# A fused attention and maxout kernel whose late output stores are cut differently

## The chip, the cores and the metric

The kernel runs on one core of one Trainium2 chip. The metric is the device time of that core in microseconds; the time before is 161.82 us, the median of three runs that lie between 161.29 and 162.05 us. The execution that was profiled took 162.39 us, and its trace spans 160.6 us of that.

## The reference

Eight batches of an attention with 32 memory slots per head (8 heads, 576 positions, head size 64), and behind it a feed-forward layer with a maximum over three products:

```python
a   = softmax(phi)                            # over the 32 slots
k_m = einsum('bhsm,bhsd->bhmd', a, k)         # 32 keys and 32 values per head
v_m = einsum('bhsm,bhsd->bhmd', a, v)
x   = softmax(q @ k_m.T / sqrt(64)) @ v_m     # [8, 8, 576, 64] -> x [4608, 512]
h   = max(max(x @ w1, x @ w2), x @ w3)        # [4608, 768]
out = h @ w_out                               # [4608, 512], float32
```

## The kernel before, in words

The weights are rewritten once. `max(x w1, x w2, x w3)` is `max(x (w1-w3), x (w2-w3), 0) + x w3`, so `w_diff` (lines 213 to 224, step `V`) subtracts `w3` from `w1` and `w2` in place in `w12`, a view of 4 x 1536 columns, in ranges of 512 columns (`BANK`). `w1` ends at column 768 (`DF`), so the range 512 to 1024 crosses the border between the two weights and is cut into two instructions there by the loop's `e`. `V0` runs on GpSimd, `V1` and `V2` on VectorE.

For each batch the attention is reduced to 32 keys and values per head, the values are folded into the weights (step `D`), and the feed-forward layer is run straight on the attention's probabilities: step `F` (`ffn1`) makes one 128-row slice of `h` transposed, step `T` (`ffn2`, lines 658 to 700) makes 128 rows of the output: six matmuls of `h` with `w_out` and two of the probabilities with the folded `w3 w_out`, summed in one PSUM bank, copied to an SBUF tile `ot` and stored to HBM. Batches 0 and 1 do four such row tiles each, and `T4` of each odd batch does 128 rows that straddle the border of the pair: the last 64 of the even batch and the first 64 of the odd one. Batch 7's `T4` is `ffn2_last` (lines 706 to 741), the last work of the kernel: its 128 rows are made in two halves of 256 columns, each copied and stored by itself, the first through VectorE and SyncE's queue (L737, L738), the second through ScalarE and its own queue (L740, L741).

Batches 2 to 7 make their other 512 rows in another way: a 2 x 2 block product with seven multiplications instead of eight. Steps `U` and `A` form sums of weight and activation blocks, and `products` (step `P`, L615) runs multiplication `i` of seven. The output has two row blocks (`r` = 0, 1; 256 rows each) and two column halves (256 columns each); multiplications 2, 4, 6 and 5 finish the four quarters (4 only when multiplication 3 is there too). Each finished quarter is written to a tile `ot` of its row block by L642 or L647. For batches 2 to 6 one store of 512 KB per row block follows once its second half is there (after 4 and after 6); for batch 7 each quarter is stored at once, 256 KB each:

```python
if n in (4, 6) or b == B - 1:        # line 648
```

The order of the work is written out by hand: the string at lines 782 to 808 is a list of steps, `name@batch`, and every engine executes its own instructions in that order. Near the end the steps that matter here are `P1@6 ... P2@6 ... P1@7 ... P2@7 P5@6 P3@6 ... P4@7 P6@6 P0@7 P5@7 P3@7 P6@7 T4@7`. The `ot` tiles come from a pool of four buffers (`opool`), so a tile's first writers wait until the stores from the tile that had this buffer before have landed. The framework puts in all semaphores. Stores and loads that are issued by SyncE or ScalarE take one of eight completion semaphores in turn; an issue first waits until the transfer that used its semaphore eight issues earlier has landed. In the built program there are 29 such issues: the two loads of `phi` at line 91, four stores of batch 0 on ScalarE's queue (`send`, line 704), 21 stores of line 700 and line 652 on SyncE's queue, and the last two, L738 and L741. At the end of the program SyncE runs nine wait instructions (line 837, the launch line, stands for them), each for two semaphores, in a fixed order; the second to the ninth hold the eight DMA semaphores in their order. A drain and a barrier over all engines follow.

Of the kernel before, what the change touches and what calls it, by code (L numbers as in the profile page):

```python
# [15 lines left out]
def kernel(  # L16
# [12 lines left out]
    nc = tc.nc  # L29

    B, H, S, D = q.shape
# [121 lines left out]
    def one_bank():  # L153
        return psum[:, int(next(banks))]
# [57 lines left out]

    def w_diff(n, swap):

        c, end = n * BANK, (n + 1) * BANK
        while c < end:
            e = min(end, (c // DF + 1) * DF)
            (nc.gpsimd if swap else nc.vector).tensor_tensor(  # L218
                out=w12[:, :, c:e],
                in0=w12[:, :, c:e],  # L220
                in1=w_sb[:, :, 2, c % DF : c % DF + e - c],
                op=ALU.subtract,
            )
            c = e
# [356 lines left out]
    def products(b, i, swap):  # L581

        s, a = sums(b), blocks(b)
        wp3 = wp3s[b]

        def plain(r, c):
            return lambda k, q: a[r][c][:, k, q]

        def summed(n):
            src = a[1][0] if n == 2 else s[min(n, 2)]  # L590
            return lambda k, q: src[:, k, q]

        def w_plain(i, j):
            c = slice(CH * j, CH * (j + 1))
            return lambda k: wo_sb[:, KT * i + k, c] if k < KT else wp3[:, i, c]

        def w_summed(n):
            return lambda k: tw[:, n, k] if k < KT else twb[b % 2][:, n]

        lhs, rhs, name = [  # L600
            (summed(0), w_summed(0), "y"),
            (plain(0, 0), w_plain(0, 0), "x"),
            (plain(0, 1), w_plain(1, 0), "z"),
            (summed(3), w_plain(1, 1), "y"),
            (summed(1), w_summed(1), "x"),
            (summed(2), w_summed(2), "x"),
            (plain(1, 1), w_summed(3), "x"),
        ][i]
        acc = quads.setdefault(b, {})
        if i < 3:  # L610
            acc[name] = one_bank()
        po = acc[name]
        for k in range(KT + 1):
            for q in range(2):
                nc.tensor.matmul(  # L615
                    po[:, q * CH : (q + 1) * CH],
                    lhsT=lhs(k, q),
                    rhs=rhs(k),
                    start=(i < 3 and k == 0 and q == 0),
                    stop=(k == KT and q == 1),  # L620
                    skip_group_check=True,
                )
        x = po.rearrange("p (q n) -> p q n", q=2)

        def copy(out_, in_):
            if swap:
                nc.vector.tensor_copy(out=out_, in_=in_)
            else:
                nc.scalar.copy(out=out_, in_=in_)  # L629

        if i in SNAP:
            t = ln if i == 0 else work.tile([P, S], FP32, name="snap", tag="r")
            t = acc[SNAP[i]] = t[:, 0:DM].rearrange("p (q n) -> p q n", q=2)
            copy(t, x)
        acc[i] = True
        done = [2] if i == 2 else [i] if i > 4 else [4] if 3 in acc and 4 in acc else []
        for n in done:
            if ("ot", n // 5) not in acc:
                acc["ot", n // 5] = opool.tile([P, 2, DM], FP32, name="ot")
            ot = acc["ot", n // 5][:, :, slice(0, CH) if n in (2, 6) else slice(CH, DM)]  # L640
            if n == 6:
                copy(ot, x)  # L642
            else:
                if n == 4:
                    x = acc["y"].rearrange("p (q n) -> p q n", q=2)
                y = acc[{2: "m1", 4: "u2", 5: "m5"}[n]]
                nc.vector.tensor_tensor(out=ot, in0=x, in1=y, op=ADD)  # L647
            if n in (4, 6) or b == B - 1:
                r0 = b * S + (b % 2) * HP
                rows = out[r0 : r0 + 2 * TW].rearrange("(q r p) c -> p q r c", q=2, r=2)  # L650
                c = slice(0, DM) if b < B - 1 else slice(0, CH) if n in (2, 6) else slice(CH, DM)
                nc.sync.dma_start(
                    out=rows[:, :, n // 5, c], in_=acc["ot", n // 5][:, :, c]
                )

    osts = {}

    def ffn2(b, t, swap):


        hT, attn = hts[b // 2], attns[b // 2]
        c0 = S - HP if t == 4 else (b % 2) * (S + HP) + t * P
        if b == B - 1:
            return ffn2_last(b, c0)
        po = one_bank()
        for n, fc in enumerate(fts[b]):
            nc.tensor.matmul(  # L667
                po,
                lhsT=hT[:, row(fc), c0 : c0 + P],
                rhs=wo_sb[:, fc, :],  # L670
                start=(n == 0),
                stop=False,
            )
        for g in range(NG):
            if t < 4:
                nc.tensor.matmul(  # L676
                    po,
                    lhsT=attn[:, g, c0 : c0 + P],
                    rhs=wp3s[b][:, g, :],
                    start=False,  # L680
                    stop=(g == NG - 1),
                )
            else:
                for u in range(2):
                    nc.tensor.matmul(  # L685
                        po[HP * u : HP * (u + 1)],
                        lhsT=attn[:, g, c0 + HP * u : c0 + HP * (u + 1)],
                        rhs=wp3s[b - 1 + u][:, g, :],
                        start=False,
                        stop=(g == NG - 1),  # L690
                        tile_position=(0, HP * u),
                    )
        ot = opool.tile([P, 2, DM], FP32, name="ot")[:, 0]
        r0 = (b // 2) * 2 * S + c0
        rows = out[r0 : r0 + P, :]
        evacuate("T", t, swap, ot, po)
        if b == 0:
            osts[t] = (rows, ot)
        else:
            nc.sync.dma_start(out=rows, in_=ot)  # L700

# [41 lines left out]
    def issue(b, n, swap):  # L743
# [29 lines left out]
            "W": lambda: w3_t(i, swap),  # L773
            "g": lambda: send(i),
            "d": lambda: fold_begin(i),
            "O": lambda: w3_o(i, swap),
            "V": lambda: w_diff(i, swap),
            "Z": lambda: warm_up(i),
# [3 lines left out]
    for w in """  # L782
# [1 line left out]
        M0@0 M1@0 R0@0 R1@0 W0@0 Y3@0 W1@0 W2@0 Z6@0 O1@0 H3@0 O3@0 O2@0 H1@0 X1@0 B1@0  # L784
        X0@0 N1@0 K1@0 O0@0 Y0@0 D1@0! D0@0! D3@0 F8@0 Y1@0 F10@0! L0@1 L1@1 F6@0 J0@1
        F0@0! F2@0! D2@0 D4@0 F4@0 F1@0 F3@0 F5@0 F11@0 F7@0 V0@0! E@1 F9@0 B0@1 N0@1
        T2@0! J1@1 Q0@1 L2@1 Q1@1 V2@0 K0@1! T1@0 S@1 B1@1 V1@0 L3@2 N1@1 M1@1 a0@1 s0@1
        R1@1 c0@1 K1@1 T3@0 D2@1 m0@1! D0@1 X1@1 L1@2 X0@1 D1@1 Q0@2 L0@2 T0@0! L2@2
        L1@3 Q1@2 L0@3 r0@2 F8@1! F4@1 F6@1! F7@1 E@2 F10@1! F2@1 F5@1 F0@1 g2@0 B@2
        D3@1 L2@3 L3@3 N@2 F9@1 F3@1 K@2! F11@1 g1@0 S@2 F1@1 D1@2! E@3 L1@4 U2@9 D0@2  # L790
        D3@2 T3@1 U0@9 T4@1! L0@4 r0@3 a@2 s@2 c@2 D2@2 B@3 L2@4 m@2! U2@2 X@2 F10@2 N@3
        F2@2 F11@2 F4@2 F0@2 K@3! L3@4 Q0@3 Q1@3 F6@2 F1@2 F8@2 g0@0 F3@2 S@3 F7@2 a@3
        F5@2 g3@0 s@3 F9@2 r0@4! E@4 U0@2 c@3 L0@5 U1@9 m@3! T2@1 X@3 U3@9 D0@3 D3@3
        T0@1! T1@1 L1@5 D2@3 B@4 D1@3! N@4 P1@2! L2@5 Q1@4 U1@2 F2@3 F6@3 F3@3 F8@3 L3@5
        U3@2 L1@6 U0@3 A0@2! Q0@4 K@4! F4@3! F0@3 F9@3 P2@2! A1@2! S@4 A2@2! A3@2! F5@3
        E@5 a@4 P4@2 F1@3 r0@5 P0@2 L2@6 F10@3 L0@6 s@4 F7@3 c@4 P5@2 m@4 D1@4! D3@4
        U1@3 F11@3 P3@2 A0@3! D2@4 B@5 A2@3! N@5 D0@4 X@4 T4@3! L1@7 A1@3! F10@4 Q0@5
        K@5 F0@4 L3@6 Q1@5 P6@2! S@5 r0@6! F11@4 F2@4! F1@4 L0@7 F6@4 F4@4! P1@3 F8@4
        a@5 s@5 U2@3 D2@5 D3@5 c@5 P2@3! E@6 m@5 A3@3! F5@4 P4@3 F3@4 F9@4 P0@3 D1@5!
        X@5 B@6 N@6 L2@7 D0@5 P5@3 U3@3 F8@5! F7@4 P3@3! r0@7! L3@7 U0@4 F2@5! F10@5 E@7  # L800
        U0@5 F3@5 Q0@6 A0@4! U1@4 P6@3 F11@5 F4@5 Q1@6 F6@5 F9@5 K@6! F0@5 A2@4! U2@4
        F5@5 S@6 F7@5 A1@4! a@6 A3@4! B@7 N@7 s@6 D3@6 D1@6! P0@4 P1@4 U3@4 K@7! P2@4!
        F1@5 Q1@7 P4@4 c@6 D0@7 D1@7 D0@6 P3@4 P5@4 U0@6 Q0@7 m@6 X@6 D2@6 D3@7 D2@7!
        A0@5! T4@5 S@7 A1@5! P6@4 F0@6 a@7 s@7 F4@6 F10@6 F1@6 c@7 F2@6 U2@5 F6@6 P1@5
        F3@6 F7@6 U1@5 P2@5 F8@6 A3@5! F9@6 F11@6 P4@5 m@7 X@7 F5@6 P0@5! F6@7 F10@7!
        A2@5! F2@7 P3@5! F4@7! F0@7 P5@5 F8@7! F1@7 F11@7 A0@6! U3@5 P6@5 F5@7 F9@7 U0@7
        A1@6 U1@7 A2@6 F3@7 U1@6 P1@6 F7@7 P0@6 P2@6! P4@6 U2@6 P1@7 A0@7 A3@6 U3@6 A1@7
        U3@7! P2@7! P5@6! P3@6 U2@7! A2@7 A3@7 P4@7 P6@6 P0@7! P5@7 P3@7! P6@7 T4@7!
    """.split():
        n, b = w.rstrip("!").split("@")  # L810
        issue(int(b), n, w.endswith("!"))
# [30 lines left out]
```

## Time and profile before

| | |
|---|---|
| median of three runs | 161.82 us (161.29 to 162.05) |
| profiled execution | 162.39 us |
| its span, first to last instruction | 160.6 us |
| TensorE matmul busy | 149.8 us, 93% |
| VectorE, ScalarE, GpSimd busy | 74%, 61%, 65% |
| granted TensorE clock | full in all 40 slices |
| DMA moved | 31.78 MB |

The span leaves out what lies before the first and after the last instruction, 1.8 us in this execution. Busy shares are averages over the whole span; what sets the end is read in the timeline and the waits of the last microseconds.

### The profile page before, as it was taken

Reading aid. Unit: us, or ns where it says so; the run is one execution under the profiler, and the core shown is the slowest. Engines: PE = TensorE matmul, PEld = TensorE weight load, DVE = VectorE, ACT = ScalarE, POOL = GpSimd, SP = SyncE. Lnnn points to the kernel's source line nnn. Section 1 sums busy time; section 2 is a strip of 40 time slices with the busy share of each in tenths; the row PEclk is TensorE's granted clock in tenths of the full one; section 3 lists DMA queues with packets and bytes.
Section 4 is the critical chain, followed back from the end, with each engine's and each line's share of the span. In section 5 each row is a group of like instructions: output and inputs, shape, how many; then the busy total and the mean of one; then the engine's idle time right before and its main releaser. Section 6 shows DMA issues by size and latency. Waiting matters only on the chain.

```text
span 160.6 us, 5165 instructions
## 1 busy us (share of the span) xinstructions
PE 149.8 (93%) x2219; PEld 100.4 (62%) x2228; DVE 118.5 (74%) x205; ACT 98.2 (61%) x140; POOL 104.3 (65%) x98
## 2 busy tenths in 40 slices
PE   7978698979897999999999999999999999999991
PEld 2433444654455537636877577787774888888871
DVE  2023803699897897897998789898989869799851
ACT  3205435742786699997777789888876944224210
POOL 7932101993039949968999996999969996910000
PEclk9999999999999999999999999999999999999999
DMA  5999999999999999999999999999803500330374
GB/s 150 164 201 203 201 209 214 279 207 212 209 276 245 276 233 261 285 262 282 268 231 209 259 260 254 261 173 170 271 0 134 196 6 0 131 131 4 150 279 159
DMA packets 22342, 31.78 MB, mean 198 GB/s; under 512 B 1072, under 2 KB 17456, under 8 KB 22320
## 3 DMA queue, kind: packets, MB, share of 16 engines
q0 software_dynamic: 16096, 21.43, 70.9%
q1 hardware_dynamic: 5504, 8.85, 15.3%
q10 hardware_dynamic: 720, 1.18, 2.2%
q8 instruction: 17, 0.28, 0.7%
q14 instruction: 5, 0.04, 0.1%
HBM read 39.32 MB, written 9.44 MB: 304 GB/s over the span
## 4 chain that ended last, share of the span: by engine, by line
PE 63%; DMA 25%; POOL 6%; issue 2%; ACT 1%; DVE 1%; POOLq 0%
PE psum L504 23%; PE psum L615 23%; DMA w_sb<-in_moe_w_dram 14%; DMA kvr<-in_v_dram 10%; PE psum L667 6%; PE psum L453 4%; PE psum L256 3%; PE psum L342 2%; POOL qq L112 1%; DMA out_dram<-ot 1%; POOL kvr L97 1%; POOL ko L97 1%; PE psum L676 1%; PE psum L685 1%; POOL w_sb L119 1%
## 5 line engine op out<-in xcount | busy, mean ns | idle before, releaser
L504 PE MATMUL psum<-hx,wp 128*128 128x288 bf16 x384 | 53.2, 286 | 0.1
L504 PEld LDWEIGHTS <-wp 128*128 128x128 bf16 x384 | 36.3, 98 | 11.6 <-issue 2.1
L517 DVE TENSOR_TENSOR hx<-psum,h 128x576 bf16<-128x576 f32 x48 | 34.8, 749 | 6.3 <-PE psum L504 4.5
L177 ACT CAST wp<-psum 128x1024 bf16<-128x1024 f32 (+1 forms) x29 | 27.5, 993 | 4.6 <-PE psum L453 4.4
L175 ACT ACTIVATE h<-psum 128x576 bf16<-128x576 f32 x34 | 21.5, 655 | 7.2 <-PE psum L504 6.6
L615 PEld LDWEIGHTS <-hx 128*128 128x128 bf16 x192 | 18.4, 98 | 3.5 <-issue 1.1
L667 PE MATMUL psum<-wo_sb,hx 128*128 128x512 bf16 x60 | 15.6, 380 | 0.3
L351 ACT ACTIVATE e<-psum 128x576 bf16<-128x576 f32 x16 | 9.5, 649 | 6.2 <-PE psum L342 6.2
L164 PE MATMUL psum<-warm 128*128 128x512 bf16 x42 | 12.0, 440 | 1.4 <-DVE warm L131 1.2
L615 PEld LDWEIGHTS <-w_sb 128*128 128x128 bf16 x120 | 11.6, 98 | 2.4 <-issue 0.8
L321 DVE STREAM_TRANSPOSE qT<-qq 128x576 f32<-128x576 f32 x16 | 11.9, 760 | 1.1 <-DMA qq<-in_q_dram 1.0
L107 POOL COPY kvr<-ko 128x2304 bf16<-128x2304 bf16 x3 | 6.3, 2111 | 8.8 <-DMA ko<-in_k_dram 8.8
L629 ACT COPY snap<-psum 128x512 f32<-128x512 f32 x11 | 6.5, 594 | 8.7 <-PE psum L615 8.7
L540 POOL TENSOR_TENSOR w_sb<-hx 128x1024 bf16<-128x1024 bf16 x5 | 10.6, 2121 | 1.6 <-DVE hx L517 1.6
L234 ACT ACTIVATE e<-ph 128x1152 bf16<-128x1152 f32 (+1 forms) x9 | 9.6, 1067 | 2.4 <-DMA ph<-in_phi_dram 2.4
L218 POOL TENSOR_TENSOR w_sb<-w_sb 128x2048 bf16<-128x2048 bf16 x1 | 4.1, 4052 | 10.6 <-PE psum L453 10.6
L179 DVE TENSOR_SCALAR h<-psum 128x576 bf16<-128x576 f32 x14 | 10.3, 746 | 0.7 <-PE psum L504 0.6
L667 PEld LDWEIGHTS <-hx 128*128 128x128 bf16 x66 | 5.9, 98 | 7.5 <-issue 1.7
L256 PEld LDWEIGHTS <-e 64*32 64x32 bf16 x720 | 7.3, 89 | 5.1 <-issue 3.6
L427 POOL TENSOR_TENSOR t<-t,sm 128x1152 bf16<-128x1152 bf16 x4 | 8.5, 2124 | 3.0 <-DVE sm L420 1.7
L540 POOL TENSOR_TENSOR twb<-wp 128x256 bf16<-128x256 bf16 x11 | 7.4, 675 | 4.2 <-ACT wp L177 4.2
L177 ACT COPY ot<-psum 128x512 f32<-128x512 f32 x9 | 5.3, 595 | 7.7 <-PE psum L676 6.8
(102 smaller groups left out, 280.6 us busy)
## 6 DMA issues: line engine op xcount, KB each, us to landing
out_dram<-ot SPq DMA_DIRECT2D x10, 512.0 KB, 3.3
qq<-in_q_dram POOLq DMA_DIRECT2D x7, 576.0 KB, 11.0
ph<-in_phi_dram POOLq DMA_DIRECT2D x7, 576.0 KB, 14.6
ko<-in_k_dram POOLq DMA_DIRECT2D x7, 576.0 KB, 16.6
kvr<-in_v_dram POOLq DMA_DIRECT2D x7, 576.0 KB, 11.1
out_dram<-ot SPq DMA_DIRECT2D x11, 256.0 KB, 6.1
w_sb<-in_moe_w_dram POOLq DMA_DIRECT2D x3, 768.0 KB, 19.0
out_dram<-ot ACTq DMA_DIRECT2D x4, 256.0 KB, 6.8
```

The lines of the kernel that those rows point to most:

```text
L164: nc.tensor.matmul(po[:, 0:BANK], lhsT=warm[:, 0:P], rhs=warm, start=True, stop=True)
L175: nc.scalar.activation(out=out_, in_=in_, func=AF.Relu)
L177: nc.scalar.copy(out=out_, in_=in_)
L179: nc.vector.tensor_scalar_max(out=out_, in0=in_, scalar1=0.0)
L234: nc.scalar.activation(out=s["e"][:, js], in_=loaded[b]["ph"][:, js], func=AF.Exp)
L256: nc.tensor.matmul(kvp[M * j : M * (j + 1), a, 0:nd], lhsT=s["e"][r, j, c, :], rhs={None: lambda: k_and_v(b, r, j, c), 0: lambda: ones_and ...
L321: nc.vector.transpose(out=s["qT"][:, j].rearrange("p j c r e -> p (j c r e)").bitcast(FP32), in_=loaded[b]["q"][:, j].rearrange("p j c d - ...
L504: nc.tensor.matmul(acc[:, h, 0:SH], lhsT=wps[b][:, g, w * DF + ft * P : w * DF + (ft + 1) * P], rhs=attn[:, g, c0 : c0 + SH], start=(g == ...
L517: nc.vector.tensor_tensor(out=hT[:, row(ft), (b % 2) * S : (b % 2 + 1) * S].rearrange("p (h n) -> p h n", h=2), in0=a, in1=s["h1", ft], op ...
L540: eng.tensor_tensor(out=out_, in0=in0, in1=in1, op=op)
L615: nc.tensor.matmul(po[:, q * CH : (q + 1) * CH], lhsT=lhs(k, q), rhs=rhs(k), start=(i < 3 and k == 0 and q == 0), stop=(k == KT and q == 1 ...
L667: nc.tensor.matmul(po, lhsT=hT[:, row(fc), c0 : c0 + P], rhs=wo_sb[:, fc, :], start=(n == 0), stop=False,)
```

## The change

Four edits. The stores of batch 6 are cut like those of batch 7: each finished quarter leaves by itself, so there are four stores of 256 KB instead of two of 512 KB. Row tile 3 of batch 1 is stored in two halves of 64 rows instead of one of 128 rows. A new step `t` (`ffn2_begin`) opens the PSUM bank of a row tile and runs the first four of its matmuls with `w_out`; `ffn2` then goes on with the rest. In the written order every `t` stands directly ahead of its own `T`. The weight difference is written as four ranges that end at the border between the weights, and `V3@0` stands directly behind `V1@0`.

```diff
     def w_diff(n, swap):
-        c, end = n * BANK, (n + 1) * BANK
+        c, end = [(0, BANK), (BANK, DF), (2 * BANK, 2 * DF), (DF, 2 * BANK)][n]
...
-            if n in (4, 6) or b == B - 1:
+            if n in (4, 6) or b >= B - 2:
                 r0 = b * S + (b % 2) * HP
                 rows = out[r0 : r0 + 2 * TW].rearrange("(q r p) c -> p q r c", q=2, r=2)
-                c = slice(0, DM) if b < B - 1 else slice(0, CH) if n in (2, 6) else slice(CH, DM)
+                c = slice(0, DM) if b < B - 2 else slice(0, CH) if n in (2, 6) else slice(CH, DM)
...
+    def ffn2_begin(b, t):
+        po = opened[b, t] = one_bank()
+        hT, c0 = hts[b // 2], (b % 2) * (S + HP) + t * P
+        for n, fc in enumerate(fts[b][0:4]):
+            nc.tensor.matmul(
+                po,
+                lhsT=hT[:, row(fc), c0 : c0 + P],
+                rhs=wo_sb[:, fc, :],
+                start=(n == 0),
+                stop=False,
+            )
...
-        po = one_bank()
-        for n, fc in enumerate(fts[b]):
+        early = (b, t) in opened
+        po = opened[b, t] if early else one_bank()
+        for n, fc in enumerate(fts[b][4 if early else 0 :]):
...
-                start=(n == 0),
+                start=(n == 0 and not early),
...
+        elif (b, t) == (1, 3):
+            for r in (slice(0, HP), slice(HP, P)):
+                nc.sync.dma_start(out=rows[r], in_=ot[r])
         else:
             nc.sync.dma_start(out=rows, in_=ot)
...
-        T2@0! J1@1 Q0@1 L2@1 Q1@1 V2@0 K0@1! T1@0 S@1 B1@1 V1@0 L3@2 N1@1 M1@1 a0@1 s0@1
+        t2@0 T2@0! J1@1 Q0@1 L2@1 Q1@1 V2@0 K0@1! t1@0 T1@0 S@1 B1@1 V1@0 V3@0 L3@2 N1@1
...
-        R1@1 c0@1 K1@1 T3@0 D2@1 m0@1! D0@1 X1@1 L1@2 X0@1 D1@1 Q0@2 L0@2 T0@0! L2@2
+        M1@1 a0@1 s0@1 R1@1 c0@1 K1@1 t3@0 T3@0 D2@1 m0@1! D0@1 X1@1 L1@2 X0@1 D1@1 Q0@2
+        L0@2 t0@0 T0@0! L2@2 L1@3 Q1@2 L0@3 r0@2 F8@1! F4@1 F6@1! F7@1 E@2 F10@1! F2@1
...
+        E@3 L1@4 U2@9 D0@2 D3@2 t3@1 T3@1 U0@9 T4@1! L0@4 r0@3 a@2 s@2 c@2 D2@2 B@3 L2@4
...
+        T2@1 X@3 U3@9 D0@3 D3@3 t0@1 T0@1! t1@1 T1@1 L1@5 D2@3 B@4 D1@3! N@4 P1@2! L2@5
```

(`t2@1` closes the line ahead of the last one shown; the rest of the string is the same list with other line breaks.)

More of the change, by code (lines that the diff above doesn't have):

```diff
@@ L654, in products @@
                 )
-    osts = {}
+    osts, opened = {}, {}
+    def ffn2_begin(b, t):
[9 more added lines that the diff above has]
+            )
     def ffn2(b, t, swap):
@@ L775, in issue @@
             "d": lambda: fold_begin(i),
+            "t": lambda: ffn2_begin(b, i),
             "O": lambda: w3_o(i, swap),
@@ L786 @@
         F0@0! F2@0! D2@0 D4@0 F4@0 F1@0 F3@0 F5@0 F11@0 F7@0 V0@0! E@1 F9@0 B0@1 N0@1
-        T2@0! J1@1 Q0@1 L2@1 Q1@1 V2@0 K0@1! T1@0 S@1 B1@1 V1@0 L3@2 N1@1 M1@1 a0@1 s0@1
-        R1@1 c0@1 K1@1 T3@0 D2@1 m0@1! D0@1 X1@1 L1@2 X0@1 D1@1 Q0@2 L0@2 T0@0! L2@2
-        L1@3 Q1@2 L0@3 r0@2 F8@1! F4@1 F6@1! F7@1 E@2 F10@1! F2@1 F5@1 F0@1 g2@0 B@2
-        D3@1 L2@3 L3@3 N@2 F9@1 F3@1 K@2! F11@1 g1@0 S@2 F1@1 D1@2! E@3 L1@4 U2@9 D0@2
-        D3@2 T3@1 U0@9 T4@1! L0@4 r0@3 a@2 s@2 c@2 D2@2 B@3 L2@4 m@2! U2@2 X@2 F10@2 N@3
@@ L792 @@
[L792 to L808, printed above, removed]
+        t2@0 T2@0! J1@1 Q0@1 L2@1 Q1@1 V2@0 K0@1! t1@0 T1@0 S@1 B1@1 V1@0 V3@0 L3@2 N1@1
@@ new lines @@
+        M1@1 a0@1 s0@1 R1@1 c0@1 K1@1 t3@0 T3@0 D2@1 m0@1! D0@1 X1@1 L1@2 X0@1 D1@1 Q0@2
+        L0@2 t0@0 T0@0! L2@2 L1@3 Q1@2 L0@3 r0@2 F8@1! F4@1 F6@1! F7@1 E@2 F10@1! F2@1
+        F5@1 F0@1 g2@0 B@2 D3@1 L2@3 L3@3 N@2 F9@1 F3@1 K@2! F11@1 g1@0 S@2 F1@1 D1@2!
+        E@3 L1@4 U2@9 D0@2 D3@2 t3@1 T3@1 U0@9 T4@1! L0@4 r0@3 a@2 s@2 c@2 D2@2 B@3 L2@4
+        m@2! U2@2 X@2 F10@2 N@3 F2@2 F11@2 F4@2 F0@2 K@3! L3@4 Q0@3 Q1@3 F6@2 F1@2 F8@2
+        g0@0 F3@2 S@3 F7@2 a@3 F5@2 g3@0 s@3 F9@2 r0@4! E@4 U0@2 c@3 L0@5 U1@9 m@3! t2@1
@@ new lines @@
+        T2@1 X@3 U3@9 D0@3 D3@3 t0@1 T0@1! t1@1 T1@1 L1@5 D2@3 B@4 D1@3! N@4 P1@2! L2@5
+        Q1@4 U1@2 F2@3 F6@3 F3@3 F8@3 L3@5 U3@2 L1@6 U0@3 A0@2! Q0@4 K@4! F4@3! F0@3
+        F9@3 P2@2! A1@2! S@4 A2@2! A3@2! F5@3 E@5 a@4 P4@2 F1@3 r0@5 P0@2 L2@6 F10@3
+        L0@6 s@4 F7@3 c@4 P5@2 m@4 D1@4! D3@4 U1@3 F11@3 P3@2 A0@3! D2@4 B@5 A2@3! N@5
+        D0@4 X@4 T4@3! L1@7 A1@3! F10@4 Q0@5 K@5 F0@4 L3@6 Q1@5 P6@2! S@5 r0@6! F11@4
+        F2@4! F1@4 L0@7 F6@4 F4@4! P1@3 F8@4 a@5 s@5 U2@3 D2@5 D3@5 c@5 P2@3! E@6 m@5
@@ new lines @@
+        A3@3! F5@4 P4@3 F3@4 F9@4 P0@3 D1@5! X@5 B@6 N@6 L2@7 D0@5 P5@3 U3@3 F8@5! F7@4
+        P3@3! r0@7! L3@7 U0@4 F2@5! F10@5 E@7 U0@5 F3@5 Q0@6 A0@4! U1@4 P6@3 F11@5 F4@5
+        Q1@6 F6@5 F9@5 K@6! F0@5 A2@4! U2@4 F5@5 S@6 F7@5 A1@4! a@6 A3@4! B@7 N@7 s@6
+        D3@6 D1@6! P0@4 P1@4 U3@4 K@7! P2@4! F1@5 Q1@7 P4@4 c@6 D0@7 D1@7 D0@6 P3@4 P5@4
+        U0@6 Q0@7 m@6 X@6 D2@6 D3@7 D2@7! A0@5! T4@5 S@7 A1@5! P6@4 F0@6 a@7 s@7 F4@6
+        F10@6 F1@6 c@7 F2@6 U2@5 F6@6 P1@5 F3@6 F7@6 U1@5 P2@5 F8@6 A3@5! F9@6 F11@6
@@ L809 @@
+        P4@5 m@7 X@7 F5@6 P0@5! F6@7 F10@7! A2@5! F2@7 P3@5! F4@7! F0@7 P5@5 F8@7! F1@7
+        F11@7 A0@6! U3@5 P6@5 F5@7 F9@7 U0@7 A1@6 U1@7 A2@6 F3@7 U1@6 P1@6 F7@7 P0@6
+        P2@6! P4@6 U2@6 P1@7 A0@7 A3@6 U3@6 A1@7 U3@7! P2@7! P5@6! P3@6 U2@7! A2@7 A3@7
+        P4@7 P6@6 P0@7! P5@7 P3@7! P6@7 T4@7!
     """.split():
```

## The prediction

> **What bounds the kernel now.** I read the page first: shares of engines, then the chain that ended last.
>
> ```profile
> span 160.6 us, 5165 instructions
> PE 149.8 (93%) x2219; PEld 100.4 (62%) x2228; DVE 118.5 (74%) x205; ACT 98.2 (61%) x140; POOL 104.3 (65%) x98
> PE 63%; DMA 25%; POOL 6%; issue 2%; ACT 1%; DVE 1%; POOLq 0%
> ```
>
> TensorE works through most of the span, so a change pays only if it shortens TensorE's stream, its stalls, or the tail behind its last matmul. The tail is in the timeline from 155 us on.
>
> ```profile
> 155.91 1.48 PE L727 MATMUL psum<-wo_sb,hx 128*128 128x256 bf16 x12
> 156.77 0.42 DVE L737 COPY ot<-psum 128x256 f32<-128x256 f32 x1 [1.56 <-PE psum L727]
> 157.22 0.34 SPq L738 DMA_DIRECT2D out_dram<-ot  x1
> 157.43 0.37 ACT L740 COPY ot<-psum 128x256 f32<-128x256 f32 x1 [1.39 <-DMA out_dram<-ot]
> 157.83 0.34 ACTq L741 DMA_DIRECT2D out_dram<-ot  x1
> ```
>
> The last matmul ends at 157.39, the last copy starts at 157.43, and the last store is issued at 157.83. (The copy's releaser is given as a store. Its two semaphore waits ran at 155.5, long before, so I read the matmul of 157.39 as the releaser.) The page's list of DMA issues gives the landing.
>
> ```profile
> out_dram<-ot SPq DMA_DIRECT2D x10, 512.0 KB, 3.3
> out_dram<-ot SPq DMA_DIRECT2D x11, 256.0 KB, 6.1
> out_dram<-ot ACTq DMA_DIRECT2D x4, 256.0 KB, 6.8
> ph<-in_phi_dram SPq DMA_DIRECT2D x2, 288.0 KB, 3.2
> out_dram<-ot SPq DMA_DIRECT2D x1, 128.0 KB, 1.7
> out_dram<-ot ACTq DMA_DIRECT2D x1, 128.0 KB, 1.7
> ```
>
> 157.83 + 1.7 is 159.53, yet the span ends at 160.6. What fills the last 1.07 us stands in the rows of the launch line: first SyncE from 157.5 to 159.0, then from 159.0 to 159.58, from 159.58 to 159.79, and from 159.79 to 159.9; then the other engines' queues after 158.
>
> ```profile
> L837 SPq EVENT_SEMAPHORE  x5: 28/28/28, 157.6 to 159.0; - x5
> ...
> L837 SPq EVENT_SEMAPHORE  x1: 28/28/28, 159.5 to 159.5; - x1
> ...
> L837 SPq EVENT_SEMAPHORE  x3: 28/28/28, 159.6 to 159.7; - x3
> ...
> L837 SPq DRAIN  x2: 7/7/7, 159.8 to 159.9; - x2
> ```
>
> ```profile
> L837 POOLq EVENT_SEMAPHORE  x4: 17/17/17, 159.9 to 160.5; - x4
> L837 ACTq DRAIN  x2: 8/80/153, 158.2 to 160.1; - x2
> ```
>
> These are SyncE's nine closing waits. Five pass by 159.0. The sixth holds the semaphore of the last store and passes at 159.5, as it lands. Three more follow, whose transfers landed long ago, and only then comes the drain at 159.8 that lets GpSimd run the barrier (159.9 to 160.5). ScalarE was through by 158.4; SyncE alone holds the barrier up. Asked in stretches of 0.01 us, the sixth wait starts between 159.54 and 159.55 and the first drain between 159.79 and 159.80: four steps in 0.25 us, 62 ns each.
>
> **The change part by part.** *Which semaphore the last store takes.* The rows above count 10 + 11 + 4 + 2 + 1 + 1 = 29 issues over eight semaphores in turn, so the last one (29 = 3 x 8 + 5) holds the fifth. After: batch 6 issues four stores for two (+2) and the split tile two for one (+1). That is 32 = 4 x 8, and the last store holds the eighth, which is in the ninth and last closing wait. The three waits behind it are then run ahead of it, while SyncE waits for the landing anyway. Gain: 3 x 62 = 0.19 us of pure tail. Nothing else covers this stretch: no engine but SyncE holds up the barrier.
>
> Each row says 28 ns, not 62; by durations alone the three would be worth 0.08 us. The Trainium skill, page "Perfetto Trace Analysis", section "Per-instruction lifecycle: what the profiler-reported window actually captures", says that of an instruction of the sequencer alone the profile shows only the execution, not its fetch, its wait or the push behind it. The trace agrees: starts lie 62 ns apart. I take the spacing.
>
> *The last store itself.* In the built program it gets a wait of its own, for the first store of batch 7 eight issues earlier. That one is the 256 KB store issued at 149.12:
>
> ```profile
> 149.12 3.70 SPq L652 DMA_DIRECT2D out_dram<-ot  x3
> ...
> out_dram<-ot SPq DMA_DIRECT2D x1, 256.0 KB, 2.1
> ...
> L740 ACTq EVENT_SEMAPHORE  x2: 17/28/38, 155.5 to 155.5; - x2
> ```
>
> It lands at 151.2, 6 us before. The wait stands between copy and store on ScalarE; L740's two waits ran at 155.5 while the copy of 155.45 to 156.03 was still busy, so the sequencer reads ahead and the new wait lies under L740's 0.37 us. Taken at 0; in line it would cost one step, 0.06. L740 gets two more semaphores (one more wait instruction), at 155.6, with ScalarE idle until 157.4: 0.
>
> *Batch 6's quarters.* SyncE issues two more stores at 0.37 us. The first goes when multiplication 2 is written, the third when 5 is; VectorE's rows give the times, SyncE is free at each.
>
> ```profile
> 145.78 0.69 DVE L647 TENSOR_TENSOR ot<-psum,snap 128x512 f32<-128x512 f32 x1 [0.19 <-issue]
> 148.40 0.69 DVE L647 TENSOR_TENSOR ot<-psum,snap 128x512 f32<-128x512 f32 x1
> 149.21 0.69 DVE L647 TENSOR_TENSOR ot<-psum,ln 128x512 f32<-128x512 f32 x1
> 150.09 0.69 DVE L647 TENSOR_TENSOR ot<-psum,snap 128x512 f32<-128x512 f32 x1 [0.18 <-PE psum L615]
> ```
>
> Stores go at 146.5, 149.1 (batch 7's, unmoved), 149.94, 150.8 and 152.4: issues of 0.37 us, at least 0.8 apart, so none queues behind another. The bytes are the same, in rows of 1 KB for 2 KB, and half of them move earlier into a stretch with hardly any traffic (DMA share 0.03):
>
> ```profile
> 146.00:149.00 3.00, 3.00 (x30) 2.70 (x28) 3.00 (x6) 1.17 (x2) 0.00 (x0) 1.00 0.03 5
> ...
> 152.00:154.00 2.00, 2.00 (x21) 1.72 (x19) 1.24 (x3) 0.42 (x1) 0.00 (x0) 1.00 0.84 332
> ```
>
> The last buffer `ot` needs batch 6's first row block landed: issued 150.8, at most 2.8 us (the 512 KB store of that place), so 153.6 against its first write at 156.77. Effect on the end: 0, between a gain (the queue empties sooner) of at most 0.1 and a loss of 0.1; I take 0 because both 128 KB stores landed in 1.7 us, the shortest of the trace.
>
> *The split tile of batch 1.*
>
> ```profile
> 60.60 14.40 SPq L700 DMA_DIRECT2D out_dram<-ot  x5
> ...
> out_dram<-ot SPq DMA_DIRECT2D x1, 256.0 KB, 6.7
> ...
> out_dram<-ot SPq DMA_DIRECT2D x1, 256.0 KB, 7.8
> ...
> 71.55 1.36 DVE L427 TENSOR_TENSOR t<-t,sm 128x1152 bf16<-128x1152 bf16 x1
> 72.83 0.68 DVE L181 COPY ot<-psum 128x512 f32<-128x512 f32 x1
> ```
>
> The store goes at 60.60 and lands at 67.3; the next (61.10) lands at 68.9. Split, the second half is issued at 60.95 and the next store slips by 0.25 to 61.35, landing about 69.2. The buffer's next writer is L181 at 72.83: 5.5 us of room. VectorE gets one more wait instruction there, under the 1.36 us of L427 ahead of it. Cost 0. The Trainium skill, page "DMA: Bandwidth & Descriptors", section "Rules for kernel authors", advises against two transfers to disjoint partition halves, since they share the same engines and serialize. Here that rule would matter only if the serializing ate the 5.5 us, which is the second rival.
>
> *Opened banks and the weight difference.* Every `t` stands right ahead of its `T`, so TensorE gets the same matmuls in the same order with the same waits: 0. `V1` before already issued two instructions, cut at column 768, and `V3` now issues the second right behind `V1`. The three pieces on VectorE stay as they are (681, 685 and 1183 ns), and so does GpSimd's 4.05 us: 0.
>
> ```profile
> L218 DVE TENSOR_TENSOR w_sb<-w_sb x3: 681/685/1183, 38.8 to 40.5; 128x1024 bf16<-128x1024 bf16 x2, 128x2048 bf16<-128x2048 bf16 x1
> L218 POOL TENSOR_TENSOR w_sb<-w_sb x1: 4052/4052/4052, 27.3 to 27.3; 128x2048 bf16<-128x2048 bf16 x1
> ```
>
> **The sum.** -0.19 us and nothing else. The profiled execution (162.39, span 160.6) would become 162.20, its span 160.4. It lies 0.57 above the median of 161.82; I take the difference over unchanged: 161.63 us, 0.12% less. The three runs before spread over 0.76 us, 0.47%, so a difference under 0.5% (0.8 us) is about what a measurement of this kernel cannot tell from none.
>
> **The rivals.** *No gain:* something else would hold the barrier as long as SyncE did. Against it, ScalarE's drain is over at 158.4 and GpSimd waits from there. Time 161.82; chance 0.10.
>
> *The halves serialize, and it is slower.* With 6.7 us each, one behind the other, the second half lands at 60.95 + 13.4 = 74.35, and L181, which writes that buffer, waits from 72.83: 1.5 us on VectorE, and TensorE behind it for the bank. Time 161.63 + 1.5 = 163.1. It decides from a landing after 72.83, that is, from 11.9 us in flight. Against it: two whole stores issued 0.5 us apart landed 1.6 us apart (67.3 and 68.9), not 6.7. Chance 0.05.
>
> *The tail's stores land sooner.* With batch 6 gone early, batch 7's would meet an emptier queue. Their 256 KB stores took 2.2 to 2.3 us against 2.1 at 149.12 in quiet: 0.1 us at best, so 161.5. Chance 0.07.
>
> **How the numbers follow.** The forecast gets the remaining 0.78. It, the first and the third rival all lie within 0.5% of before. Faster by over 0.5% (below 161.0) needs noise on top of the gain: the lowest run lay 0.53 under its median, and 161.63 - 0.53 = 161.1, so 0.05. Slower by over 0.5% (above 162.6) is the second rival: 0.05. Same: 0.90. The range goes from 161.1 to the first rival plus the upper scatter (161.82 + 0.23), rounded up to 162.1; it leaves out the second rival.
>
> **What would show it.** Right: in the closing waits, the one of 159.5 is the ninth, and the drain follows 62 ns behind it, with the barrier unchanged; the last store still takes 1.7 us; TensorE's last matmul still ends at about 157.4. Wrong: waits behind the last landing, L181 idle for a store, a last store issued more than 0.04 us after its copy, or TensorE's end moved by more than the few tenths that executions differ.

## The result and the profile after

The changed kernel takes 161.19 us against 161.80 us for the kernel before, medians of 22 runs each. The ratio is 0.9959 with a 95% interval of 0.9939 to 0.9978: 0.4% less, somewhere between 0.36 and 0.99 us. Two of the changed kernel's runs, with a granted clock of 0.989, took 163.2 us; such runs count in the medians and not in the ratio. The forecast was 161.63 us, 0.19 us less than before. The direction is as forecast. The time lies in the range too, but by luck: the range's lower bound of 161.1 us came from the scatter of single runs. 0.19 us (a ratio of 0.9988) lies outside the interval: more was gained than the sum has terms for.

The profiled execution of the changed kernel took 160.59 us, its span is 158.8. Its tail, in the timeline (start, duration):

```profile
154.27 1.49 PE L744 MATMUL psum<-wo_sb,hx 128*128 128x256 bf16 x12
155.13 0.42 DVE L754 COPY ot<-psum 128x256 f32<-128x256 f32 x1 [1.56 <-PE psum L744]
155.59 0.34 SPq L755 DMA_DIRECT2D out_dram<-ot  x1
155.79 0.37 ACT L757 COPY ot<-psum 128x256 f32<-128x256 f32 x1 [1.39 <-PE psum L744]
156.19 0.34 ACTq L758 DMA_DIRECT2D out_dram<-ot  x1
```

The steps from the last matmul to the last store are those of before, to the hundredth: copy 0.04 us behind the matmul, store 0.40 us behind the copy's start. SyncE's closing waits (rows of the launch line, in four stretches of time) are the ones that moved:

```profile
L856 SPq EVENT_SEMAPHORE  x6: 27/28/28, 156.0 to 156.3; - x6
...
L856 SPq EVENT_SEMAPHORE  x2: 28/28/28, 156.6 to 157.4; - x2
...
L856 SPq EVENT_SEMAPHORE  x1: 28/28/28, 157.9 to 157.9; - x1
...
L856 SPq DRAIN  x1: 7/7/7, 158.0 to 158.0; - x1
```

The ninth wait passes when the last store lands (157.9), and the drain follows at once. In stretches of 0.01 us the drain starts 1.78 us behind the issue of the last store; before it was 159.80 - 157.83 = 1.97. The difference, 0.18 us when both are read to the nanosecond, is the 0.19 us of the forecast.

The two profiled spans differ by 1.8 us, far more than the timed medians. Most of that (1.3 us) is already there when batch 2's scores are read, at 55.1 us before and 53.8 us after, in a part of the program in which the change leaves every engine's instructions as they were. The traces of the other kernels differ there by as much, and two traces with the same instructions by 1.1 us (55.1 before, 54.0 with the store edits undone, the first experiment below). From there on the two traces run in step to about 0.01 us, with one exception, on VectorE around the scores of batch 6. Before, in the timeline:

```profile
110.62 0.76 DVE L517 TENSOR_TENSOR hx<-psum,h 128x576 bf16<-128x576 f32 x1
...
112.14 1.42 DVE L517 TENSOR_TENSOR hx<-psum,h 128x576 bf16<-128x576 f32 x2 [0.76 <-PE psum L342]
...
112.95 0.46 PE L256 MATMUL psum<-kvr,e 64*32 64x130 bf16 x33 [0.28 <-DVE hx L517]
```

After, the same instructions (VectorE's rows, then TensorE's):

```profile
109.33 0.76 DVE L517 TENSOR_TENSOR hx<-psum,h 128x576 bf16<-128x576 f32 x1
110.48 0.76 DVE L517 TENSOR_TENSOR hx<-psum,h 128x576 bf16<-128x576 f32 x1 [0.39 <-PE psum L504]
111.48 0.76 DVE L517 TENSOR_TENSOR hx<-psum,h 128x576 bf16<-128x576 f32 x1 [0.25 <-PE psum L504]
...
111.31 0.81 PE L256 MATMUL psum<-kvr,e 64*32 64x130 bf16 x72
```

From one `L517` to the next it is 1.51 us before and 1.15 us after, and TensorE's `L256` of the next step waits for VectorE in the first and not in the second. The wait that VectorE holds ahead of that instruction had long passed, in the rows of line 517 of the kernel before:

```profile
L517 DVEq EVENT_SEMAPHORE  x1: 21/21/21, 111.7 to 111.7; - x1
L517 DVE TENSOR_TENSOR hx<-psum,h x1: 757/757/757, 112.1 to 112.1; 128x576 bf16<-128x576 f32 x1
```

In the trace's own resolution the wait ends at 111.73 and the instruction starts at 112.14. In the changed kernel that step takes 0.04 us. The 0.37 us are a pause that no semaphore in the trace explains. The releaser that the view names, the matmul of `L342`, is only the last one to have ended. The `L517` itself also waits for ScalarE, but not for the `L175` that ended last there, at 111.86: in the changed kernel the same `L517` starts at 110.48, ahead of the end of that `L175` at 110.57. The time from the first score of batch 6 to that of batch 7 (ScalarE's `L351`) is 124.31 - 112.18 = 12.13 us before and 122.67 - 110.89 = 11.78 after. These 0.35 us and the 0.18 of the tail make 0.53 us, a ratio of 0.9967, inside the interval.

### The profile page after: what moved, and what is told of

Read it like the earlier page. It is cut to its first block, busy times and chain, and to the rows that moved or that the text cites. A ratio compares the mean times of both kernels' runs of the same rounds, so it can differ in the third digit from the quotient of the medians.

```text
span 158.8 us, 5173 instructions
## 1 busy us (share of the span) xinstructions
PE 150.0 (94%) x2219; PEld 100.1 (63%) x2228; DVE 118.4 (75%) x205; ACT 98.3 (62%) x140; POOL 104.4 (66%) x98
## 4 chain that ended last, share of the span: by engine, by line
PE 65%; DMA 23%; POOL 6%; issue 2%; ACT 1%; POOLq 0%
PE psum L504 24%; PE psum L615 24%; DMA w_sb<-in_moe_w_dram 14%; DMA kvr<-in_v_dram 10%; PE psum L453 4%; PE psum L681 4%; PE psum L256 3%; PE psum L663 2%; PE psum L342 2%; POOL qq L112 1%; POOL kvr L97 1%; POOL ko L97 1%; PE psum L690 1%; PE psum L699 1%; POOL w_sb L119 1%
## 5 line engine op out<-in xcount | busy, mean ns | idle before, releaser
L517 DVE TENSOR_TENSOR hx<-psum,h 128x576 bf16<-128x576 f32 x48 | 34.9, 750 | 6.1 <-PE psum L504 5.0
L175 ACT ACTIVATE h<-psum 128x576 bf16<-128x576 f32 x34 | 21.5, 656 | 7.6 <-PE psum L504 7.0
L615 PEld LDWEIGHTS <-hx 128*128 128x128 bf16 x192 | 18.4, 98 | 3.5 <-issue 1.1
L164 PE MATMUL psum<-warm 128*128 128x512 bf16 x42 | 12.6, 455 | 1.4 <-DVE warm L131 1.2
L351 ACT ACTIVATE e<-psum 128x576 bf16<-128x576 f32 x16 | 9.5, 649 | 6.0 <-PE psum L342 6.0
L179 DVE TENSOR_SCALAR h<-psum 128x576 bf16<-128x576 f32 x14 | 10.3, 745 | 0.7 <-PE psum L504 0.6
L615 PE MATMUL psum<-wo_sb,hx 128*128 128x256 bf16 x72 | 9.8, 273 | 0.0
L615 PE MATMUL psum<-w3T,hx 128*128 128x256 bf16 x72 | 9.8, 273 | 0.0
L427 POOL TENSOR_TENSOR t<-t,sm 128x1152 bf16<-128x1152 bf16 x4 | 8.5, 2136 | 1.6 <-DVE sm L420 1.0
L647 DVE TENSOR_TENSOR ot<-psum,snap 128x512 f32<-128x512 f32 x12 | 8.2, 684 | 1.8 <-PE psum L615 1.1
```

The costliest lines, as they stand in the source:

```text
L164: nc.tensor.matmul(po[:, 0:BANK], lhsT=warm[:, 0:P], rhs=warm, start=True, stop=True)
L175: nc.scalar.activation(out=out_, in_=in_, func=AF.Relu)
L179: nc.vector.tensor_scalar_max(out=out_, in0=in_, scalar1=0.0)
L351: nc.scalar.activation(out=e2[:, a].rearrange("p (t r c) -> p t r c", t=2, c=NC), in_=sc[a][:, :, 0:SH].rearrange("p t (c r) -> p t r c", ...
L427: (nc.vector if swap else nc.gpsimd).tensor_tensor(out=t, in0=t, in1=x.to_broadcast(list(t.shape)), op=ALU.mult,)
L517: nc.vector.tensor_tensor(out=hT[:, row(ft), (b % 2) * S : (b % 2 + 1) * S].rearrange("p (h n) -> p h n", h=2), in0=a, in1=s["h1", ft], op ...
```

## The experiments

Two theories were set against each other. The *closing-wait theory* is the forecast's: only the number of closing waits behind the last store counts, 62 ns each. The *stream-position theory* was formed after the first four experiments, from their traces and the trace after: VectorE pauses at one place of its instruction stream, the 192nd instruction that the trace shows, whatever instruction stands there; the split tile gives VectorE one more wait instruction at 72 us, so the pause falls on another one. In the kernel before, the 192nd is the `L517` that could have started. In the changed kernel it is a wait instruction that TensorE holds up for longer than the pause: it runs 0.32 us behind the end of the instruction ahead, where a wait whose semaphore is already there runs 0.08 us ahead of that end.

**The store edits undone.** Only the opened banks and the new ranges of the weight difference stay.

```diff
-            if n in (4, 6) or b >= B - 2:
+            if n in (4, 6) or b == B - 1:
...
-        elif (b, t) == (1, 3):
-            for r in (slice(0, HP), slice(HP, P)):
-                nc.sync.dma_start(out=rows[r], in_=ot[r])
```

> The two edits of the stores are undone; the opened banks and the four ranges of the weight difference stay. Closing-wait theory (all that counts is how many closing waits stand behind the one that holds the last store, 62 ns each): three stand behind it as before, ratio to before 1.000, and the span from the last landing to the first drain 0.25 us. Theory that an opened bank or the weight difference moves TensorE's stream: ratio below 1, up to the 0.4% of the whole change. Theory that two loadings of one program differ by some tenths of a per cent: any ratio between 0.997 and 1.003 with the tail as before.

Ratio 1.0001 (0.9979 to 1.0024), last store to drain 1.97 us, batch 6 to batch 7 12.14 us: as before in all three. Its trace has the same instructions as that of the kernel before, engine by engine (addresses are not in the traces), so it also shows what two loadings of one program differ by.

**The change again,** unaltered.

> The whole change once more, for the size of its effect on this chip. Closing-wait theory: ratio 0.9988 (0.19 us less), the drain 0.06 us behind the last landing in place of 0.25. Theory that something ahead of the tail gains too: 0.996 again, with TensorE's last matmul some 0.4 us earlier than in the kernel of the first run of this call.

Ratio 0.9959 (0.9940 to 0.9978), 161.03 against 161.74 us; last store to drain 1.80, batch 6 to batch 7 11.78. The gain ahead of the tail is there a second time.

**Batch 6's quarters alone.**

```diff
-            if n in (4, 6) or b == B - 1:
+            if n in (4, 6) or b >= B - 2:
...
-                c = slice(0, DM) if b < B - 1 else slice(0, CH) if n in (2, 6) else slice(CH, DM)
+                c = slice(0, DM) if b < B - 2 else slice(0, CH) if n in (2, 6) else slice(CH, DM)
```

> Only batch 6's stores are cut into quarters: 31 issues, so the last store takes the seventh semaphore and one closing wait stands behind it. Closing-wait theory: 0.12 us less than before, ratio 0.9992, drain 0.12 us behind the last landing. Theory that the early departure of batch 6 is what gains: about the whole 0.4%, ratio 0.996.

Ratio 0.9981 (0.9960 to 1.0002). Last store to drain 1.86 us, 0.11 less than before, as one wait behind in place of three should give. Batch 6 to batch 7 takes 12.13 us, as before, and from the scores of batch 7 to the last matmul it is 33.07 us against 33.08. The early departure itself moved nothing in the trace; the interval is too wide to tell the 0.12 us of the waits from the 0.31 us that was measured.

**Three halved tiles in place of the quarters.**

```diff
+        elif b == 1 and t in (3, 4, 2):
+            for r in (slice(0, HP), slice(HP, P)):
+                nc.sync.dma_start(out=rows[r], in_=ot[r])
```

> Batch 6 stays in 512 KB stores; in its place three row tiles of batch 1 (3, 4 and 2) are stored in two halves each: 32 issues, the last store on the eighth semaphore. Closing-wait theory: the same 0.19 us as the whole change, ratio 0.9988, drain 0.06 us behind the last landing. Theory that batch 6's early departure gains: ratio 1.000 less the 0.1% of the semaphore. Theory that halves of 64 rows serialize (6.7 us each): VectorE's or ScalarE's copies at 72 to 74 us wait, ratio up to 1.01.

Ratio 0.9987 (0.9971 to 1.0003), last store to drain 1.80: the semaphore gives its gain without batch 6 (from the last landing to the drain 0.08 us in place of 0.26). But batch 6 to 7 took 11.81 us and batch 5 to 6 18.78, where every kernel above has 18.58. VectorE has two more wait instructions here, and the pause stands at the 192nd instruction again, which now is the `L517` ahead of the former one. This trace is what the stream-position theory was made from, so it is no test of it; those that follow are.

**The split tile alone.**

```diff
+        elif (b, t) == (1, 3):
+            for r in (slice(0, HP), slice(HP, P)):
+                nc.sync.dma_start(out=rows[r], in_=ot[r])
```

> Only row tile 3 of batch 1 is stored in halves: 30 issues, two closing waits behind the last store, and one more wait instruction on VectorE at 72 us (ahead of the copy of row tile 2). Closing-wait theory alone: 0.06 us less, ratio 0.9996. Stream-position theory (VectorE pauses some 0.4 us at one fixed place of its instruction stream, its 192nd traced instruction, and the extra wait moves that place from an instruction that could start to one that has to wait anyway): 0.35 us more, 0.41 in all, ratio 0.9975, and no idle VectorE at batch 6's scores where before had 0.43 us.

The trace has what the stream-position theory asked for: 11.78 us from batch 6 to batch 7, no pause, last store to drain 1.91. The timing, 0.9996 (0.9973 to 1.0019), does not tell 0.9975 from 1.

**One VectorE instruction more, nothing else.** The step `v` is put in ahead of `N@4`.

```diff
+            "v": lambda: nc.vector.memset(warm[:, 0:1], 0.0),
...
-        T0@1! T1@1 L1@5 D2@3 B@4 D1@3! N@4 P1@2! L2@5 Q1@4 U1@2 F2@3 F6@3 F3@3 F8@3 L3@5
+        T0@1! T1@1 L1@5 D2@3 B@4 D1@3! v@4 N@4 P1@2! L2@5 Q1@4 U1@2 F2@3 F6@3 F3@3 F8@3 L3@5
```

> The kernel before with one tiny memset more on VectorE (one column of a tile that is no longer used), put in at 75 us where VectorE waits for TensorE; stores and semaphores as before. Stream-position theory: 0.35 us less, ratio 0.9978, the tail with its three closing waits unchanged, and the interval between the scores of batch 6 and batch 7 12.13 us down to 11.78. Closing-wait theory, and any theory that needs the stores: ratio 1.000 (at worst 60 ns more for the memset).

Ratio 0.9980 (0.9955 to 1.0005), 161.28 against 161.62 us. The timeline of VectorE shows the gap of 1.15 us of the changed kernel, with stores and semaphores as before and 1.97 us from the last store to the drain:

```profile
109.35 0.76 DVE L517 TENSOR_TENSOR hx<-psum,h 128x576 bf16<-128x576 f32 x1
110.50 0.76 DVE L517 TENSOR_TENSOR hx<-psum,h 128x576 bf16<-128x576 f32 x1 [0.40 <-PE psum L504]
111.50 0.76 DVE L517 TENSOR_TENSOR hx<-psum,h 128x576 bf16<-128x576 f32 x1 [0.24 <-PE psum L504]
```

Batch 6 to 7 takes 11.78 us. So 0.35 us go without any store being touched.

**The change and that instruction,** so that VectorE's stream is shifted by two.

> The whole change plus the same memset: VectorE's stream is shifted by two against before. Stream-position theory: the pause falls on an instruction that could start again (as in the kernel with three halved tiles, where it cost about 0.2 us), so ratio 0.998 and 0.2 us slower than the change alone; the drain stays 0.06 us behind the last landing. Closing-wait theory alone: as the change, 0.9959.

Ratio 0.9984 (0.9959 to 1.0010). The pause is back, one `L517` earlier than in the kernel before:

```profile
107.83 0.72 DVE L517 TENSOR_TENSOR hx<-psum,h 128x576 bf16<-128x576 f32 x1
...
109.58 1.53 DVE L517 TENSOR_TENSOR hx<-psum,h 128x576 bf16<-128x576 f32 x2 [0.36 <-ACT h L175]
111.58 0.76 DVE L517 TENSOR_TENSOR hx<-psum,h 128x576 bf16<-128x576 f32 x1 [0.47 <-PE psum L504]
```

The releaser that the view names, ScalarE's `L175`, is again only the last one to have ended, at 109.36: in the changed kernel the same `L517` starts at 109.33 and that `L175` ends at 109.48. Nor is it GpSimd: one of its instructions runs from 108.46 to 110.58, right across the pause. Batch 5 to 6 takes 18.79 us, 0.2 more than in the changed kernel, and the tail is the changed kernel's (1.80). One instruction more takes 0.35 us away or gives 0.2 back, by where it moves the pause.

**One issue too many:** the change with a second halved tile.

```diff
-        elif (b, t) == (1, 3):
+        elif b == 1 and t in (3, 4):
```

> The whole change with a second halved tile (row tile 4 of batch 1): 33 issues, so the last store wraps to the first semaphore, which is in the second closing wait; seven stand behind it. Closing-wait theory: first drain 0.50 us behind the last landing in place of 0.06, so 0.43 us slower than the change; against before 0.25 slower from this and, if the stream-position theory holds too, 0.35 faster from that: ratio 0.9994. If closing waits cost nothing when their transfers are long done: ratio 0.996 as the change.

The last store wraps to the first semaphore. Its issue and the closing waits (before the landing: one, not shown; then in two stretches):

```profile
157.14 0.34 ACTq L758 DMA_DIRECT2D out_dram<-ot  x1
...
L856 SPq EVENT_SEMAPHORE  x7: 27/28/28, 158.9 to 159.2; - x7
...
L856 SPq EVENT_SEMAPHORE  x1: 28/28/28, 159.3 to 159.3; - x1
L856 SPq DRAIN  x1: 7/7/7, 159.4 to 159.4; - x1
```

The wait that holds the last store passes at 158.9 and seven more are run one by one behind it: 2.21 us from the last store to the drain, 0.43 more than with the change. Batch 6 to 7 is 11.79 us, since VectorE's stream is that of the change. Both terms together were expected at 0.9994, and 0.9994 (0.9973 to 1.0014) was measured. That the two agree to the last digit is luck with an interval this wide, but 0.996, the time if closing waits cost nothing, lies outside it.

**The memset at the start of VectorE's stream.**

```diff
     nc.vector.memset(warm, 0.0)
+    nc.vector.memset(warm[:, 0:1], 0.0)
```

> The kernel before with the tiny memset put at the very start of VectorE's stream (behind the first memset), so every later instruction is shifted by one. If the pauses belong to places in the stream, both stay at their places, ahead of the 65th and the 192nd traced instruction, which are now other instructions: the first falls on the instruction that stood ahead before, the second is covered as with the memset at 75 us, the interval between the scores of batches 6 and 7 is 11.78 us, and the ratio 0.998. If the second pause came from something at 75 to 112 us (the moved wait, the memset's place), it stays as before: 12.13 us, ratio 1.000.

Half of it held. Batch 6 to 7 takes 11.78 us, so the extra instruction does at the start what it does at 75 us. The other half fell: what had looked like a first pause, at 47 us, moved with its instruction (0.48 us between a wait and the first `L179`, now the 66th instruction and on line 180, before the 65th). It is no pause: VectorE is busy there with the transpose ahead, which ends at 47.8 while the next instruction starts at 47.7. One such place is shown, not two. Ratio 0.9986 (0.9953 to 1.0018).

**The split tile alone, again.**

> Row tile 3 of batch 1 in halves once more, since the first timing (0.9996, 0.9973 to 1.0019) could not tell 0.9975 from 1. Stream-position theory: 0.9975, the interval between the scores of batches 6 and 7 11.78 us, first drain 0.2 us behind the last landing. Closing-wait theory alone: 0.9996.

Ratio 0.9990 (0.9962 to 1.0017), last store to drain 1.91, batch 6 to 7 11.84 us at a mean clock of 0.989. Again the trace shows the step and the timing doesn't reach it.

All the traces side by side, in us. The last column is the time from batch 4's first score to the end of the span:

| kernel | VectorE shifted by | 5 to 6 | 6 to 7 | closing waits behind | last store to drain | batch 4 to end |
|---|---|---|---|---|---|---|
| before | 0 | 18.58 | 12.13 | 3 | 1.97 | 79.44 |
| store edits undone | 0 | 18.58 | 12.14 | 3 | 1.97 | 79.46 |
| quarters alone | 0 | 18.58 | 12.13 | 1 | 1.86 | 79.34 |
| split tile alone (twice) | 1 | 18.57, 18.57 | 11.78, 11.84 | 2 | 1.91, 1.91 | 79.02, 79.09 |
| memset at 75 us | 1 | 18.57 | 11.78 | 3 | 1.97 | 79.10 |
| memset at the start | 1 | 18.57 | 11.78 | 3 | 1.97 | 79.10 |
| the change (twice) | 1 | 18.58, 18.58 | 11.78, 11.78 | 0 | 1.78, 1.80 | 78.93, 78.93 |
| one issue too many | 1 | 18.57 | 11.79 | 7 | 2.21 | 79.35 |
| three halved tiles | 2 | 18.78 | 11.81 | 0 | 1.80 | 79.15 |
| change and memset | 2 | 18.79 | 11.79 | 0 | 1.80 | 79.17 |

The last column adds up from the two terms: with the memset alone it is 0.34 us less than before, with the quarters alone 0.10, with the change 0.50. So behind batch 4 no third term of more than some hundredths is left. The times can't show this split: the split tile alone (twice) and the two memsets on the kernel before were expected at 0.9975 to 0.998 and gave 0.9980 to 0.9996, and the change gave 0.9959 twice where the sum says 0.9967. Every expected value lies within its interval, but a small third term ahead of batch 4, where the traces scatter, is not excluded.

No kernel here beats the change: it already has both, no closing wait behind and the pause covered.

## Why the prediction was right, and where it was not

*The last store's semaphore.* Right in mechanism and size. The distance from last store to drain falls with the waits behind it, 2.21, 1.97, 1.91, 1.86 and 1.79 us for seven, three, two, one and none: 0.42 us for seven, 60 ns each against 62 forecast. That the last store has the same latency, 1.70 us, also held.

*The new wait of the last store on ScalarE* cost nothing: the store follows the copy's start by 0.40 us before and after.

*Batch 6's quarters.* Taken at 0 at the end. The traces bear that out: from batch 7's scores to the last matmul 33.07 to 33.09 us in every kernel. The rival that the tail's stores land sooner fell: batch 7's stores of 256 KB took 2.13 to 2.29 us before and 2.15 to 2.32 after, and the last store 1.70 us in both.

*The opened banks and the weight difference.* 0, as forecast: the kernel that has only these has the same instructions in its trace as the kernel before, and took 1.0001 of its time (0.9979 to 1.0024).

*The split tile.* Here the prediction failed. It said of the extra wait instruction on VectorE "under the 1.36 us of L427 ahead of it. Cost 0". The instruction itself is hidden there, as said. But it shifts every later instruction of VectorE by one, and that moved a pause of 0.37 us off an instruction that TensorE waited for: 0.35 us gained, at 112 us, 40 us behind the instruction that did it. The prediction looked for the effect of an instruction only where it is executed. The sum was short by this term: 0.19 + 0.35 = 0.54 us, 0.9967, against 0.9959 (twice) measured.

*The halves serialize.* Fell. They landed 5.7 and 6.0 us after their issue (5.6 to 6.9 us in the other traces), the whole tile before after 6.7, and VectorE's copy into that buffer did not wait. In the rows of the changed kernel:

```profile
L715 SPq DMA_DIRECT2D out_dram<-ot x2: 533/560/587, 59.3 to 59.9; - x2
...
DMA to landing us min/median/max: 5.7/5.8/6.0
```

The issues took 0.53 and 0.59 us of SyncE, not the 0.35 that was taken over from whole tiles; SyncE has nothing else to do there.

*The range and the chances.* Three runs had put the scatter at 0.47%. With 22 a difference of 0.4% shows, so the bound of 0.5% was a rough one. One of the signs was set too tight: TensorE's last matmul ends at 155.75 us after, 1.64 us sooner and far more than the "few tenths that executions differ". 1.31 us of that lie ahead of batch 2's scores, where traces differ by up to 1.4 us, and 0.35 us are the pause.

## What to carry to other kernels

Where a kernel ends with a row of closing waits, count the transfers: the last one's place in the turn of semaphores sets how many waits are run behind its landing, and a cut or joined store anywhere in the kernel moves it. An added or removed instruction, even a bare wait, shifts the rest of its engine's stream; so when a small edit gains or loses some tenths of a microsecond far from where it stands, compare the two traces interval by interval and look for a pause that no semaphore explains. A kernel with one idle instruction more in the same stream tells such a shift from the edit's own effect.

## What the runs showed of the hardware that was not expected

VectorE pauses for 0.37 us at a fixed place of its stream, the 192nd traced instruction, in all five traces where that place falls on an instruction that could start (shifts of 0 and 2). In the seven with a shift of 1 a wait instruction stands there, and the pause cannot be seen. What makes it is not shown. The Trainium skill, page "Runtime: NRT & Kernel Launch", section "Instruction fetch mechanics", says that an engine's instructions are refilled in blocks of 256 and that crossing a block's border is mostly hidden. A border would be at home at a fixed place like this one. But how many instructions that the trace does not show stand ahead of the 192nd was not counted, and no run here moved the border by itself, so that the pause is such a crossing stays open; and hidden it was only where a wait stood in its place. The traces list transfers of the kind "instruction" (17 of 16 KB and five of 8 KB in the kernel before), but not for which engine. In four of the five traces with the pause none of them runs during it; in the fifth, the change and the memset, one of 16 KB does (108.88 to 110.10 us). So a wait for such a transfer isn't seen either.

Also unexpected is that the early part of the kernel, up to batch 2's scores, differs by up to 1.4 us between executions (53.7 to 55.1 us in these traces), while from batch 4's scores on everything but the pause repeats to a few hundredths. (Between batches 2 and 4 two traces took longer, by 0.35 us with the store edits undone and by 0.14 us with the split tile the second time.) This is why single timings told so little here: steps of 0.06 to 0.35 us are plain in the traces and hardly reach out of the intervals of the times.
